# Another order for the last expert selection of an attention-then-MoE kernel, with one row group scaled by ScalarE

## The chip, the cores and the metric

The kernel runs on one core of a Trainium2 chip. The metric is the device time of one execution in microseconds (us); the time before is the median of three runs, 466.85 us (466.36 to 467.3). TensorE, VectorE, ScalarE and GpSimd compute; SyncE issues most DMAs, GpSimd the indirect ones (gathers and scatters by token number). In the profile they are PE (PEld for its weight loads), DVE, ACT, POOL and SP.

## What is computed

Causal attention over 8 batches, 12 heads, 448 tokens and head width 64, whose result (3584 tokens of 768 numbers) goes into a mixture of 8 experts. Each token picks one expert by the largest logit; an expert keeps the 80 tokens with the largest gate weight (its capacity) and drops the rest; a kept token gives its row times two matrices with a ReLU between, times its gate weight. All other output rows are zero.

```python
scores = scale * np.matmul(q, k.transpose(0, 1, 3, 2))      # then the causal mask
attn = np.exp(scores - max) / sum
x = (attn @ v), heads side by side                          # (3584, 768)
logits = x @ w_gate                                         # (3584, 8)
expert_idx = np.argmax(logits, axis=1)
gate_w = softmax(logits)[arange, expert_idx]
for e in range(8):
    tok_idx = the tokens with expert_idx == e, at most the 80 of the largest gate_w
    h = np.maximum(x[tok_idx] @ w1[e], 0.0)
    out[tok_idx] = gate_w[tok_idx, None] * (h @ w2[e])
```

## The kernel before

The work has three stages. The attention stage goes through 48 head pairs (8 batches of 6) in a software pipeline of 8 slots a pair; while one batch's heads are computed, the selection of the batch before it is spread over the slots. The expert stage takes the 8 experts one after the other: it gathers an expert's 80 rows from `xs` (the attention result in HBM), transposes them on TensorE, splits weights and rows into a high and a low half of 16 bits, and multiplies. A few chunks of the weights are not split but multiplied in 32 bits ("whole"); for expert 0 these are chunks 3 to 5 of the first matrix, and they come first.

Between the two lies the **tail**: the last batch has no attention left beside it, so its selection runs alone. Its order is written out by hand in the string `TAIL` (line 43): the names are taken from left to right, each calls one step, and each engine executes what the steps put into its queue in that order. The names that matter here:

- `r0w` to `r7w`: three TensorE transposes that turn a row group (128 or 64 tokens x 384 columns) of the last batch into rows (`row_group`, line 592). `r0e` to `r7e`: take them out of the accumulator banks. `r0m` to `r7m`: the scaling by the softmax's reciprocal sums, where another engine does it. One letter each in `ROW_ENGINES` (line 49) says who scales: `v` VectorE in one instruction (line 611), `a` ScalarE in six, one for each head (line 605), `p` a ScalarE copy (line 607) and then GpSimd (line 619). Scaled rows are written to `xs` by a DMA from SyncE's queue (line 615). Groups 3 and 7 are the ones of 64 tokens.
- `lg`, `logit`, `shifted`, `chosen`, `sums`, `one_hot`, `wsum`, `one_zero`, `wmore`, `weight`, `weighted`: logits, their maximum, the exponentials (`gex`, line 646, in the step `chosen`, on ScalarE), the one-hot of the expert and the gate weight, else on VectorE. `rest`: the left-over steps of the batch before, among them `tab` and `row` (lines 873 and 881, small ScalarE copies).
- `r0t`, `r0c`, `r1t`, `r1c`: one-hots and weights are transposed on TensorE (`selt`, line 731) and copied to `ex` by ScalarE (line 734).
- `rl`, `lt`, `cp`, `ro`: compare the 80 weights kept so far for each expert with those of the batch (lines 761, 767), count (line 774, "the counts' product") and make ranks (line 779).
- `c3w` to `c0w`: products that spread the batch's weights over 512, 384, 256 and 128 columns (`rn`, line 745); `c3l` to `c0l`: the comparisons on VectorE (`less`, line 748); `gt3` to `gt0`: counts of them (line 813).
- `places`, `places_more`, `earlier`, `own`, `rank`, `rr`, `tn`, `tab`: the one-hots of the places (`rm`, line 794), the tokens' ranks (`rank`, `rr`, lines 820 to 849), and the products `tn` (lines 859, 862) that sort token numbers and weights into the table. Out of it come `idx` (line 923), the token numbers for the gathers, and `gws`, the weights.
- `*n`: n matrix products without use (`wp`, line 1108) that keep TensorE busy.

Behind the tail ScalarE has eight weight splits in its queue (`wh`, line 1180), then `xw` and `xh` (lines 1220 and 1222), the gathered rows of expert 0 taken from the transposes `xtp` (line 1215). The first expert product (`hp`, line 1237) reads `xw`. The first gather (line 1197) waits for `idx` and for all writes to `xs`.

Of the kernel before, what the change touches and what calls it, by code (L numbers as in the profile page):

```python
# [41 lines left out]

TAIL = """
u ta ya tb yb v0 td yd tc yc v1 vy guard invert last_rows w gp0 wy close piece gp1 gs
r0w r0e r1w lp r1e r1m rest rest r2w r2e r3w r3e lg logit shifted chosen rest rest r4w r4e r5w *2
sums one_hot wsum one_zero wmore columns r0t r0c *3 weight weighted parts hold rl r1t r1c *1 lt r3m r4m r5e r5m cp ro r6w r6e r6m
c3w c3l c2w r7w r7e r7m c2l c1w gt3 *2 c0w c1l gt2 *1 c0l *1 gt1 places *1 earlier gt0 places_more own *5 rank rr tn tab *20
"""
ROW_ENGINES = "vpappppp"


@with_exitstack
def attention_then_moe(
# [928 lines left out]
    with tc.manual_schedule():  # L982
# [121 lines left out]
        def keep_warm(times):  # L1104

            wp = ps_v.tile([P, S], F32, name="wp", tag="xp")
            for _ in range(times):
                nc.tensor.matmul(wp, identb, before[:, 0:S], start=True, stop=True)
        for i, x in enumerate(ROW_ENGINES):
            g, t = divmod(i, NT)  # L1110
# [331 lines left out]
```

## Time and profile before

| | |
|---|---|
| median of three runs | 466.85 us (466.36 to 467.3) |
| the profiled execution | 466.07 us, span 464.2 us |
| TensorE busy, in the span | 441.8 us (95%) |
| VectorE, ScalarE, GpSimd busy | 413.1, 392.4, 310.3 us |
| DMA | 120.84 MB, mean 260 GB/s |
| TensorE from 340 to 350 us of the span | 9.55 us busy, clock 1.00, DMA share 0.27 |
| TensorE from 360 to 370 us | 10.00 us busy, clock 1.00, DMA share 1.01 |
| tail: last row transposes of the attention stage to the first expert product | 328.89 to 350.84 us |

Times inside the span count from its first instruction. In a timeline row stand start, length, engine, line, operation, names (out<-in), shapes and how many; in brackets follows how long the engine stood idle before it and who released it. Lengths of neighbours overlap by a little, so the distance of two starts is what an instruction costs in a queue; the length says when its result is there.

### The profile page before, as it was taken

The page shows a single profiled execution, that of the slowest core. Times are in us where ns is not written, and L with a number is a line of the kernel's source. Part 1 is how long each engine was busy: PE and PEld are TensorE (multiplying, and loading weights), DVE is VectorE, ACT ScalarE, POOL GpSimd, SP SyncE. Part 2 cuts the span into 40 slices and gives each one's busy share as a digit, 9 for nine tenths or more (in the row PEclk, how much of TensorE's full clock was granted, in tenths as well). Part 3 has the DMA queues.
Part 4 walks back from the last instruction along what each step waited for, and adds up shares of the span by engine and source line. Part 5 has one row for each costly group of instructions (what it writes and reads, how often), then busy time and mean ns, then how long its engine had stood idle before and what let it go on. Part 6 is the DMA issues. An engine that isn't in the chain of part 4 may idle for free.

```text
span 464.2 us, 14187 instructions
## 1 busy us (share of the span) xinstructions
PE 441.8 (95%) x4981; PEld 346.8 (75%) x4981; DVE 413.1 (89%) x1285; ACT 392.4 (85%) x1077; POOL 310.3 (67%) x382
## 2 busy tenths in 40 slices
PE   4899999999999999999999999999989999999994
PEld 2566667866777786677777767777648999999994
DVE  6888899988998999899899989989579999999892
ACT  6898989878988997898889789888586989988792
POOL 7999999988987987898798789860145133410011
PEclk9999999999999999999999999999999999999999
DMA  7758899989769578966957997539937999999941
GB/s 221 185 153 238 249 262 299 280 248 306 202 207 305 161 232 259 265 182 213 297 165 225 264 260 200 178 129 373 413 130 254 399 390 395 394 422 423 424 163 44
DMA packets 42998, 120.84 MB, mean 260 GB/s; under 512 B 6146, under 2 KB 23810, under 8 KB 39472
## 3 DMA queue, kind: packets, MB, share of 16 engines
q1 hardware_dynamic: 41712, 116.21, 76.9%
q0 software_dynamic: 1056, 3.51, 2.4%
q8 instruction: 39, 0.64, 0.6%
q14 instruction: 31, 0.25, 0.2%
q10 hardware_dynamic: 160, 0.23, 0.2%
HBM read 96.36 MB, written 23.99 MB: 259 GB/s over the span
## 4 chain that ended last, share of the span: by engine, by line
PE 83%; DVE 6%; DMA 3%; ACT 3%; issue 2%; SPq 1%; POOLq 0%; DVEq 0%
PE xp L495 16%; PE tp L465 15%; PE sp L423 6%; PE sp L424 5%; PE rt L592 4%; PE op L1245 4%; PE op L1237 4%; PE hp L1237 3%; PE gp L545 3%; PE hp L1252 3%; PE hp L1251 3%; PE hp L1249 3%; PE sp L433 3%; DMA qk<-k_t 3%; DVE ns L445 2%
## 5 line engine op out<-in xcount | busy, mean ns | idle before, releaser
L448 ACT ACTIVATE prob<-ns,nb 128x128 f32<-128x128 f32 (+3 forms) x336 | 177.0, 529 | 22.6 <-DVE nb L445 20.1
L445 DVE CUSTOM_DVE_ANT_0 ns<-sp,mask 128x384 f32<-128x384 f32 (+2 forms) x288 | 116.0, 413 | 18.7 <-PE sp L424 14.7
L465 PE MATMUL tp<-ident,prob 128*128 128x128 f32 x768 | 118.1, 276 | 0.9 <-ACT prob L448 0.9
L477 ACT COPY PT<-tp 128x512 f32<-128x512 f32 x182 | 104.0, 572 | 17.5 <-PE sp L423 8.4
L395 POOL TENSOR_TENSOR qk<-qk,qk 128x448 f16<-128x448 f32 x92 | 97.3, 1080 | 13.1 <-DVE qk L387 7.4
L465 PEld LDWEIGHTS tp<-ident,prob 128*128 128x128 f32 x768 | 89.6, 142 | 11.4 <-ACT prob L448 1.9
L1165 DVE SCALAR_TENSOR_TENSOR wl<-wraw,wh 128x768 f16<-128x768 f32 (+1 forms) x91 | 92.0, 1067 | 2.5 <-ACT wh L1180 2.3
L495 PE MATMUL xp<-PT,vt 128*64 128x448 f32 (+3 forms) x768 | 91.2, 380 | 0.0
L495 PEld LDWEIGHTS xp<-PT,vt 128*64 128x64 f32 x768 | 53.8, 137 | 42.7 <-issue 22.6
L423 PE MATMUL sp<-qk 128*128 128x384 f16 (+2 forms) x288 | 75.8, 279 | 8.0 <-DVE qk L349 5.1
L1180 ACT ACTIVATE wh<-wraw 128x768 f16<-128x768 f32 (+1 forms) x91 | 78.9, 931 | 4.2 <-PE hp L1252 1.8
L424 PE MATMUL sp<-qk 128*128 128x384 f16 (+2 forms) x288 | 78.1, 277 | 1.6 <-DVE qk L349 0.8
L448 ACT ACTIVATION_READ_ACCUMULATOR prob<-ns,nb 128x1 f32 x336 | 63.9, 190 | 0.0
L1338 POOL DMA_INDIRECT out<-yo,idx x8 | 14.6, 1828 | 69.0 <-ACT yo L1335 65.1
L390 POOL TENSOR_TENSOR qk<-qk,qk 64x448 f16<-64x448 f32 x46 | 54.2, 1179 | 3.4
L391 POOL TENSOR_TENSOR qk<-qk,qk 64x448 f16<-64x448 f32 x46 | 51.0, 1108 | 3.2
L387 DVE CAST qk<-qk 128x896 f16<-128x896 f32 x46 | 41.2, 897 | 1.1 <-DMA qk<-k_t 1.1
L423 PEld LDWEIGHTS <-qk 128*128 128x128 f16 x288 | 28.5, 99 | 17.1 <-issue 8.6
L384 POOL CAST qk<-qk 64x896 f16<-64x896 f32 x40 | 37.4, 936 | 4.3 <-PE sp L436 3.1
L1249 PEld LDWEIGHTS <-wh 128*128 128x128 f16 x362 | 36.5, 101 | 0.0
L1251 PEld LDWEIGHTS <-wh 128*128 128x128 f16 x362 | 36.2, 100 | 0.0
L1252 PEld LDWEIGHTS <-wl 128*128 128x128 f16 x362 | 36.2, 100 | 0.0
(192 smaller groups left out, 926.8 us busy)
## 6 DMA issues: line engine op xcount, KB each, us to landing
wraw<-w SPq DMA_DIRECT2D x27, 1536.0 KB, 20.4
qk<-k_t SPq DMA_DIRECT2D x92, 224.0 KB, 5.9
out<-mask_l SPq DMA_DIRECT2D x56, 192.0 KB, 4.4
qk<-q_t SPq DMA_DIRECT2D x23, 448.0 KB, 4.4
vt<-v_t SPq DMA_DIRECT2D x24, 384.0 KB, 5.9
xs<-xr SPq DMA_DIRECT2D x42, 192.0 KB, 3.9
wraw<-w SPq DMA_DIRECT2D x24, 256.0 KB, 6.1
vt<-v_t SPq DMA_DIRECT2D x24, 64.0 KB, 5.5
```

Of the source, the lines that this page charges most:

```text
L390: nc.gpsimd.tensor_tensor(out=qa[hi, i], in0=qf[lo, i], in1=qa[lo, i], op=ALU.subtract)
L391: nc.gpsimd.tensor_tensor(out=qb[lo, i], in0=qf[hi, i], in1=qb[hi, i], op=ALU.subtract)
L395: nc.gpsimd.tensor_tensor(out=k_lo[j][:, i], in0=kf[j][:, i], in1=k_hi[j][:, i], op=ALU.subtract)
L423: nc.tensor.matmul(sp[:, 0:w], qx[:, p, t * P:w], kx[:, p, 0:w], start=True, stop=False)
L424: nc.tensor.matmul(sp[:, 0:w], qx[:, p, t * P:w], lx[:, p, 0:w], start=False, stop=True)
L445: pr.masked = nc.vector.tensor_tensor_reduce(out=ns[:, 0:w], in0=sp[:, 0:w], in1=m, scale=-1.0 / 8.0, scalar=HUGE, op0=ALU.add, op1=ALU.mi ...
L448: nc.scalar.activation(pr.P[:, off:off + w], ns[:, 0:w], AF.Exp, bias=nb, scale=-1.0, accum_out=total)
L465: nc.tensor.transpose(pr.tp[:, i], pr.P[:, off:off + P], ident)
L477: copy(dst, src)
L495: state["pe"] = nc.tensor.matmul(xp[rows, 0:w], st["vt"][:, c, p * P + j * DH:p * P + (j + 1) * DH], pr.PT[:, j, n0:n0 + w], start=(c == 0 ...
L1165: return nc.vector.scalar_tensor_tensor(out=l, in0=src, scalar=SW, in1=h, op0=ALU.mult, op1=ALU.subtract)
L1180: nc.scalar.activation(h, src, AF.Copy, scale=SW)
```

## The change

Three things change in the hand-written order and one letter in `ROW_ENGINES`. The steps up to `chosen` come before the copies of row groups 2 and 3. The 512 columns' product and comparison come before the counts, and row groups 4 and 5 before both. The last row group, of 64 tokens, is scaled by ScalarE, in six instructions, instead of copied by ScalarE and scaled by GpSimd. Beside these the row groups 2, 3, 6 and 7 stand elsewhere, the comparison of 384 columns follows `ro`, the second `rm` and the first stand together behind `earlier`, and there are 40 products without use where there were 36. The core of the diff (its other lines are further names of the order):

```diff
-c3w c3l c2w r7w r7e r7m c2l c1w gt3 *2 c0w c1l gt2 *1 c0l *1 gt1 places *1 earlier gt0 places_more own *5 rank rr tn tab *20
+ro r6w r6e r6m c1w r7w r7e c2l *1 gt3 c0w c1l *1 gt2 *1 c0l gt1 earlier places gt0 places_more own *7 rank rr tn tab *20
...
-ROW_ENGINES = "vpappppp"
+ROW_ENGINES = "vpappppa"
```

On ScalarE, in the tail, from the small copy of the left-over step `tab` to the weight splits (`xrl` are the rows, `gex` the exponentials, `ex` the turned one-hots and weights, `wh` the splits), before:

```order
L873 CAST tab_0_678<-tn 80x40
L605 ACTIVATE xrl<-rt,sums 128x64 x6
L607 COPY xrl<-rt 64x384
L646 ACTIVATE gex<-gsh 128x32
L881 COPY row_0_682<-rp_6296 24x80
L607 COPY xrl<-rt 128x384
L734 COPY ex<-selt 24x512 x2
L607 COPY xrl<-rt 128x384 x2
L607 COPY xrl<-rt 64x384
L1180 ACTIVATE wh<-wraw 128x1024 x8
```

The same stretch of ScalarE's queue now:

```order
L873 CAST tab_0_678<-tn 80x40
L646 ACTIVATE gex<-gsh 128x32
L881 COPY row_0_682<-rp_6282 24x80
L605 ACTIVATE xrl<-rt,sums 128x64 x6
L734 COPY ex<-selt 24x512
L607 COPY xrl<-rt 64x384
L734 COPY ex<-selt 24x512
L607 COPY xrl<-rt 128x384 x3
L605 ACTIVATE xrl<-rt,rql 64x64 x6
L1180 ACTIVATE wh<-wraw 128x1024 x8
```

The exponentials stand ahead of the six scalings of group 2 and the copy of group 3; this copy stands between the two `ex` copies, the copies of groups 4, 5 and 6 behind the second; and where the copy of group 7 stood last, six scalings of 64x64 stand.

On TensorE, from the second `selt` to the counts (`rt` are row transposes, `rn` the columns' products, `cp` the counts, `wp` the products without use), the difference:

```order
 L731 MATMUL selt<-identb,mv 128x128
+L592 MATMUL rt<-ident,xu 128x128 x6
 L1108 LDWEIGHTS identb
 L1108 MATMUL wp<-before,identb 128x448
+L745 LDWEIGHTS ex
+L745 MATMUL rn<-ex 128x512
 L774 LDWEIGHTS lt
 L774 MATMUL cp<-oh_674,lt 80x8
```

And directly behind the last of the four `cp`:

```order
 L774 MATMUL cp<-oh_674,lt 80x8
-L592 MATMUL rt<-ident,xu 128x128 x3
-L745 LDWEIGHTS ex
-L745 MATMUL rn<-ex 128x512
 L745 LDWEIGHTS ex
 L745 MATMUL rn<-ex 128x384
```

The 512-column product moved from behind the four counts, and behind a row group, to ahead of them; row groups 4 and 5 moved ahead of it. Row group 6 now follows the 384-column product and row group 7 the 256-column one. On VectorE the 512-column comparison stands ahead of `ro`, and both `rm` behind the sum of `earlier`. SyncE's queue is the same, and GpSimd's lacks its fifth scaling.

More of the change, by code (lines that the diff above doesn't have):

```diff
@@ L44 @@
 u ta ya tb yb v0 td yd tc yc v1 vy guard invert last_rows w gp0 wy close piece gp1 gs
-r0w r0e r1w lp r1e r1m rest rest r2w r2e r3w r3e lg logit shifted chosen rest rest r4w r4e r5w *2
-sums one_hot wsum one_zero wmore columns r0t r0c *3 weight weighted parts hold rl r1t r1c *1 lt r3m r4m r5e r5m cp ro r6w r6e r6m
-c3w c3l c2w r7w r7e r7m c2l c1w gt3 *2 c0w c1l gt2 *1 c0l *1 gt1 places *1 earlier gt0 places_more own *5 rank rr tn tab *20
+r0w r0e r1w lp r1e r1m rest rest r2w lg logit shifted chosen rest rest r2e *3
+sums one_hot wsum one_zero wmore columns *3 r0t r0c r3w r3e *3 weight weighted parts hold rl r1t r1c r4w r5w *1 lt c3w r3m r4e r4m r5e r5m c3l cp c2w
+ro r6w r6e r6m c1w r7w r7e c2l *1 gt3 c0w c1l *1 gt2 *1 c0l gt1 earlier places gt0 places_more own *7 rank rr tn tab *20
 """
-ROW_ENGINES = "vpappppp"
+ROW_ENGINES = "vpappppa"
 @with_exitstack
```

## The prediction

> **What bounds the kernel now.** I read the page first, then the chain of waits from 322 us on, then who waited for whom in the expert stage, and last the engines' timelines between 333 and 352 us, where every edit lies.
>
> ```profile
> span 464.2 us, 14187 instructions
> ```
>
> The profiled execution took 466.07 us: this span and 1.87 us around it. It lies 0.78 us under the median of the runs shown (466.85). The sum below is a difference, so I add it to either.
>
> The chain of waits at the hand-over from the last selection to the experts (start, length, what):
>
> ```profile
> 346.51 0.16 DVE idx L923
> ...
> 346.96 3.17 DMA xg<-xs,idx
> ...
> 350.26 0.60 PE xtp L1215 x6
> 350.86 5.57 PE hp L1237 x48
> ```
>
> The list of token numbers (idx) releases the first gather, the gather releases the transposes of its rows, and these release the first expert product. From 350 us to the end TensorE waits for almost nothing; these are the only rows of its matmuls in the list of waits of that stretch (total, times, longest):
>
> ```profile
> PE xtp L1215 <- DMA xg<-xs,idx: 0.2, 1, 0.2
> ...
> PE ytp L1331 <- DVE yt L1311: 0.2, 1, 0.2
> ```
>
> So the expert stage is bound by TensorE, and what moves the first product, now at 350.86, moves the end by as much. The question is only what releases it. In the chain it is idx and the gather. But the product also needs xw, which ScalarE makes from the transposes, and ScalarE's queue reads (start, length, line, names, shapes, idle time before and its releaser):
>
> ```profile
> 336.01 1.34 ACT L605 ACTIVATE xrl<-rt,sums 128x64 f32<-128x64 f32 x6 [0.18 <-PE rt L592]
> 337.21 0.48 ACT L607 COPY xrl<-rt 64x384 f32<-64x384 f32 x1
> 337.57 0.25 ACT L646 ACTIVATE gex<-gsh 128x32 f32<-128x32 f32 x1
> 337.70 0.20 ACT L881 COPY row<-rp 24x80 bf16<-24x80 bf16 x1
> ...
> 340.21 0.57 ACT L734 COPY ex<-selt 24x512 bf16<-24x512 bf16 x1 [0.68 <-PE selt L731]
> 340.70 0.46 ACT L607 COPY xrl<-rt 128x384 f32<-128x384 f32 x1
> ...
> 342.30 0.47 ACT L607 COPY xrl<-rt 64x384 f32<-64x384 f32 x1 [0.22 <-PE rt L592]
> 342.67 7.68 ACT L1180 ACTIVATE wh<-wraw 128x1024 f16<-128x1024 f32 x8
> 350.55 0.44 ACT L1220 ACTIVATE xw<-xtp 128x80 f32<-128x80 f32 x2 [0.20 <-PE xtp L1215]
> ```
>
> Two things are to be seen. The exponential (L646) stands behind seven row operations. And between the last row copy and xw stand eight weight splits without a gap, after which ScalarE idles 0.20 us. That is all its slack: a second path, almost as late as the gather.
>
> **The exponential ahead of the rows.** VectorE's rows around it and on to the ranks:
>
> ```profile
> 336.65 0.19 DVE L641 TENSOR_TENSOR gsh<-logit,gmx 128x32 f32<-128x32 f32 x1
> ...
> 337.32 0.19 DVE L659 TENSOR_TENSOR goh<-goh,gfm 128x32 f32<-128x32 f32 x1
> 337.85 0.18 DVE L665 TENSOR_REDUCE ggw<-gex 128x4 f32<-128x32 f32 x1 [0.34 <-ACT gex L646]
> ...
> 339.46 0.19 DVE L716 TENSOR_TENSOR mv<-grest,mv 128x32 bf16<-128x32 f32 x1
> ...
> 341.21 0.22 DVE L779 TENSOR_SCALAR ro<-cp,pnum 80x8 f16<-80x8 f32 x1 [0.29 <-PE cp L774]
> 341.81 0.75 DVE L748 SCALAR_TENSOR_TENSOR less<-rn,ggw,before 128x512 bf16<-128x512 f32 x1 [0.38 <-PE rn L745]
> ...
> 343.43 0.34 DVE L748 SCALAR_TENSOR_TENSOR less<-rn,ggw,before 128x128 bf16<-128x128 f32 x1
> 343.70 0.08 DVE L748 DVE_READ_ACCUMULATOR less<-rn,ggw,before 128x1 f32 x1
> 343.70 0.48 DVE L794 TENSOR_TENSOR rm<-ro,slots_e 80x320 bf16<-80x320 f16 x1
> ...
> 345.40 0.49 DVE L849 TENSOR_TENSOR rr<-rank,slots_t 128x320 bf16<-128x320 f16 x1
> ```
>
> gsh ends at 336.84; the exponential can begin some 0.04 later and end by 337.13, before VectorE is through with L659 at 337.51. The 0.34 us wait goes; the one-hots and all that follow come 0.34 earlier, L716 (what the second selt reads) ending at 339.31. What is late next is TensorE, by its own queue:
>
> ```profile
> 338.53 0.40 PE L731 MATMUL selt<-identb,oh 128*128 128x128 bf16 x4 [1.13 <-DVE oh L702]
> 338.76 0.73 PE L1108 MATMUL wp<-before,identb 128*128 128x448 bf16 x3
> 339.59 0.32 PE L761 MATMUL rl<-row,ex 128*128 128x80 bf16 x4
> 339.79 0.38 PE L731 MATMUL selt<-identb,mv 128*128 128x128 bf16 x4
> 340.01 0.35 PE L1108 MATMUL wp<-before,identb 128*128 128x448 bf16 x1
> 340.31 0.86 PE L774 MATMUL cp<-oh,lt 128*80 128x8 bf16 x4
> 341.03 0.53 PE L592 MATMUL rt<-ident,xu 128*128 128x128 f32 x3
> 341.39 0.54 PE L745 MATMUL rn<-ex 128*128 128x512 bf16 x2
> 341.77 0.49 PE L592 MATMUL rt<-ident,xu 128*128 128x128 f32 x3
> ```
>
> Pitches, from one start to the next: 0.23 for four selt, 0.36 for three row transposes, 0.20 for four rl; three wp end 0.73 after their start against 0.35 for one, so 0.19 each. The first selt starts at 338.53 - 0.34 = 338.19. Three row transposes are now put behind it, so rl follows at 338.19 + 0.23 + 0.36 + 3 x 0.19 = 339.35 (before 339.59): 0.24 is left of the 0.34. The six scalings of the third row group now stand between exponential and first ex copy: 336.88 + 0.23 for the two small operations, then 1.20 (336.01 to 337.21), free at 338.31; selt is there at 338.59. They are hidden by 0.3 us; without that cover they would cost what exceeds it.
>
> **The 512 columns ahead of the counts.** The second selt runs at 339.55 and its ex copy ends at 339.55 + 0.38 + 0.04 + 0.57 = 340.54 (the copy of a row group between the two ex copies ends by 339.6). TensorE meanwhile does two row groups and one wp, 339.55 + 0.22 + 2 x 0.36 + 0.19 = 340.68, and takes the 512-column product then, not at 341.39: 0.71 earlier. The first comparison moves from 341.81 to 341.10. Two things are given back. The ranks ro (0.22 long) now lie behind it: 0.10, taken midway between nothing (wholly overlapped) and its length. And the sum after the last comparison has no rm to cover its accumulator read any more (rm started at 343.70, the read ended at 343.78): 0.12 with the hand-over. So rr starts at 345.40 - 0.71 + 0.10 + 0.12 = 344.91 and the gather 0.49 earlier. The wp in front of tn, seven where there were five, begin when the last comparison is done, about 343.2, and are through by 344.7, before rr ends. The gather's transposes would start at 349.77 and, were they the last thing, the product at 350.37.
>
> **The last row group on ScalarE.** Where its transposes stand on TensorE: the 512- and the 384-column product took 0.38 together (341.39 to 341.77), the counts take some 0.22 when VectorE no longer paces them (estimate from the four rl), three transposes 0.36, the 256-column product some 0.11 by its share of the 0.38: 340.68 + 0.38 + 0.22 + 0.36 + 0.11 = 341.75, against 341.77 now. So ScalarE gets the last row group when it did, at 342.28. Then, in place of one copy after which the next instruction started 0.37 later (342.30 to 342.67), come six scalings. The trace has none of 64x64; the nearest row is the 128x64 one, 1.20 for six. Half the partitions do not help: 64x384 and 128x384 copies take 0.48 and 0.46. Bounds are six times 0.32 without any overlap, 1.9, and half the row's price, 0.6. I take 1.20: the weight splits begin at 343.48, 0.81 later, and xw, the ninth in that queue, is reached 0.81 later too. Of this the 0.20 idle time and some 0.10 of overlap between neighbours (the copy ended at 342.77, the split began at 342.67) are covered: xw starts at 351.06 where it was 350.55, and the first product about 351.37. **The path has changed hands: the gather comes 0.49 earlier, the product 0.51 later.** The two price bounds make it -0.1 and +1.2.
>
> The Trainium skill, page "ScalarE: Activation LUTs", section "What ACT_TABLE_LOAD costs", gives an ACTIVATE with one pointer operand 280 ns + 0.833 ns per column, neighbours overlapping by 93 ns; an estimate from it is 0.24 a piece, 1.44 for six, and the sum would be 0.75 where the rows give 0.51. Its "Rules for kernel authors" sends multiplications to VectorE and not to ScalarE, which speaks against this edit; the trace's 0.20 is a little cheaper than the page's figure.
>
> **GpSimd and the row writes.** GpSimd loses its fifth scaling:
>
> ```profile
> 340.44 2.54 POOL L619 TENSOR_TENSOR xrl<-xrl,sums 128x384 f32<-128x384 f32 x3
> 342.94 0.82 POOL L619 TENSOR_TENSOR xrl<-xrl,rql 64x384 f32<-64x384 f32 x1
> 346.96 1.08 POOL L1197 DMA_INDIRECT xg<-xs,idx  x1 [3.19 <-DVE gws L930]
> ...
> DMA to landing us min/median/max: 1.8/1.9/1.9
> ...
> xs<-xr SPq DMA_DIRECT2D x42, 192.0 KB, 3.9
> ```
>
> These are two stretches of its timeline and the gather, the landing times of the eight row writes of this stage, and the page's row for the earlier row writes. Now its chain of three ends at 342.98 and the write of the last row group follows 343.76. Afterwards the three start when their first copy is done, about 340.95, and end at 343.5; the last scaling ends at 342.28 + 1.34 = 343.62. The two last writes go out of SyncE's queue at 343.5 and about 343.85: the last as now. At the 1.9 us that these eight writes took, it lands at 345.75, and the gather, which waits for it, needs it at 346.18. Hidden, by 0.4 us where it was 0.9.
>
> **Rivals.** *The gather's path still decides.* If ScalarE reached xw by 350.06, the product would follow the transposes: -0.49, 466.36 us. The six scalings would have to cost no more than the copy did, and the eight splits to run 0.5 shorter, as they could if part of their 7.68 is waiting that the trace does not tell from work; with the first alone it is about -0.3. For it: the chain of now runs through idx. Against: the 1.20 in the row and splits that follow each other every 0.96. 0.10. *The row writes decide.* If the last write takes the 3.9 us of the earlier row writes (last row above) instead of 1.9, it lands at 347.75 and the gather starts 0.3 later, 348.05, against 346.96: +1.1, 467.95 us, slower. It decides from a landing of 2.3 us on. For it: the write is the last of eight and its slack is halved. Against: all eight took 1.8 to 1.9. 0.08. *The gain and the delay are lost in the expert stage,* its queue of splits absorbing the shift, so that 466.85 stays: 0.10; against it, TensorE has no gap there that could take it up.
>
> **The numbers.** The forecast, xw held up by ScalarE's queue, has 0.72: +0.5, that is 466.57 against the profiled 466.07, and 467.35 against the median 466.85, or +0.11%. A measurement of this kernel can tell about 0.2% (0.93 us) from no change. The forecast (to about +0.8 with a late last transpose), the first and the third rival lie mostly within it. Slower takes the second rival and the tail of the forecast, 0.13; faster only what a lucky set of runs would add to the first rival, 0.04; same 0.83. The range takes in the first rival with half the spread of the runs below it, and the second above: 466.1 to 468.0.
>
> **What would show it.** Right: the exponential right behind gsh and no wait at L665; the 512-column comparison near 341.1; idx about 0.5 earlier; six L605 of 64x64 before the splits; xw released not by the transposes but by the splits, with TensorE idle about 1 us between the gather's transposes and the first product. Wrong: a first product before 350.86, or a gather that waits for the row writes.

## The result, and the profile after

The changed kernel takes 471.78 us (median of 6 runs, 470.41 to 472.54), the kernel before 467.08 us beside it (6 runs, 466.01 to 468.74): a ratio of 1.0095, 95% interval 1.007 to 1.012. It is slower by some 4.4 us, where 467.35 was forecast, at most 468.0. The profiled execution took 470.71 us; the page:

```profile
span 468.9 us, 14200 instructions
```

**Where the time went.** First the table of stretches, TensorE's busy time in three of them (stretch, length, then busy time and count of PE, PEld, DVE, ACT and POOL, the clock, the DMA share and GB/s). Before:

```profile
350.00:356.00 6.00, 5.81 (x53) 5.63 (x53) 5.36 (x6) 4.00 (x8) 3.44 (x2) 1.00 0.85 296
356.00:362.00 6.00, 6.00 (x159) 6.00 (x159) 5.84 (x9) 4.13 (x8) 1.17 (x1) 1.00 1.01 343
362.00:372.00 10.00, 10.00 (x165) 10.00 (x161) 10.00 (x14) 9.86 (x17) 1.74 (x1) 1.00 1.01 397
```

After:

```profile
350.00:356.00 6.00, 4.48 (x41) 4.34 (x41) 3.97 (x5) 5.09 (x9) 4.43 (x3) 1.00 0.77 264
356.00:362.00 6.00, 3.83 (x69) 3.71 (x69) 3.49 (x5) 1.26 (x3) 0.96 (x1) 1.00 0.99 285
362.00:372.00 10.00, 9.23 (x205) 9.08 (x202) 10.00 (x12) 9.08 (x15) 0.00 (x0) 1.00 1.02 388
```

TensorE idles 1.52 + 2.17 + 0.77 = 4.46 us in these 22 us, where it idled 0.19. The loss is three gaps behind the selection, at the clock of before; nothing in the selection itself has become longer. TensorE's rows at these places and the last entries of the list of waits:

```profile
351.56 0.61 PE L1215 MATMUL xtp<-ident,xg 80*128 80x80 f32 x6 [1.52 <-ACT wh L1180]
352.14 5.59 PE L1237 MATMUL hp<-xw,wraw 128*128 128x80 f32 x48
359.90 0.61 PE L1215 MATMUL xtp<-ident,xg 80*128 80x80 f32 x6 [2.17 <-DMA xg<-xs,idx]
```

```profile
PE xtp L1215 <- DMA xg<-xs,idx: 2.2, 1, 2.2
...
PE hp L1237 <- issue: 0.8, 1, 0.8
```

The first gap, ahead of the first expert's transposes, is put down to a weight split of ScalarE, the eighth, which ends at 351.45. But in the kernel before the transposes started at 350.26, while the eighth split still ran (342.67 + 7.68 = 350.35), so they don't need it. What they wait for is the landing of the first gather's rows, 0.14 us ahead of them in both kernels (350.12 and 351.42). The second gap is the second expert's gather; the third stands in the second expert's products and waits for nothing that the profile shows.

**The selection did what was forecast.** VectorE's rows after (start, length, line, names, shapes, idle before):

```profile
338.00 0.18 DVE L665 TENSOR_REDUCE ggw<-gex 128x4 f32<-128x32 f32 x1
...
341.44 0.75 DVE L748 SCALAR_TENSOR_TENSOR less<-rn,ggw,before 128x512 bf16<-128x512 f32 x1 [0.32 <-PE rn L745]
...
346.48 0.16 DVE L923 TENSOR_TENSOR idx<-xf,tn 80x8 int32<-80x8 f32 x1
...
346.96 0.16 DVE L931 TENSOR_TENSOR gws<-gws,sv 80x8 f32<-80x8 f32 x1
347.15 3.50 DVE L1165 SCALAR_TENSOR_TENSOR wl<-wraw,wh 128x1024 f16<-128x1024 f32 x3
```

The two executions differ by 0.58 us ahead of the first changed name of the order, which no changed code explains. The start of the gate product shows it, first before, then after:

```profile
332.23 1.74 PE L545 MATMUL gp<-xu,wgd 128*32 128x448 f32 x12
```

```profile
332.81 1.70 PE L545 MATMUL gp<-xu,wgd 128*32 128x448 f32 x11
```

So in what follows "from the gate product" is the start minus 332.23 before, and minus 332.81 after; the experiments use each run's own start. L665 no longer waits. The 512-column comparison starts at 8.63 (before 9.58), idx at 13.67 (before 14.28): 0.61 earlier, where 0.49 was forecast. VectorE's first weight split (`wl`, L1165) follows this list at 14.34, also 0.61 earlier (before 347.18, 14.95).

**The gather did not come earlier by as much.** GpSimd after, and beside it the second gather of before (its first stands in the prediction):

```profile
347.29 2.03 POOL L1197 DMA_INDIRECT xg<-xs,idx  x1 [3.49 <-DVE gws L931]
349.63 1.84 POOL L1197 DMA_INDIRECT xg<-xs,idx  x1 [0.31 <-issue]
```

```profile
348.34 0.96 POOL L1197 DMA_INDIRECT xg<-xs,idx  x1 [0.31 <-issue]
```

The first gather starts at 14.48 from the gate product, where it was 14.73: 0.25 earlier, not 0.61. It takes 2.03 us, not 1.08, and the second starts 0.71 us later from the gate product (16.82, before 16.11; 1.29 later in the span). The row names `gws` as the releaser, which had ended before; where several are waited for, the records tell them apart. The records of GpSimd's sequencer, finer than the views, show when its wait for the last row write ends. Before, that is at 345.89, idx is done at 346.67, and the gather starts 0.29 behind idx. After, the row write's wait ends at 346.33, idx is done at 346.64, and the gather starts 0.96 behind the row write. The same 0.96 stands in other runs, such as the one with the unscaled rows below (346.11 to 347.07). So before, the row write was hidden by 0.11 us only (345.89 + 0.96 = 346.85, against 346.96). The row write is the 96 KB one in the DMA view of the changed kernel (342 to 348 us; issues, KB each, us to landing):

```profile
xs<-xrl SPq DMA_DIRECT2D x3, 192.0 KB, 1.8
xs<-xrl SPq DMA_DIRECT2D x1, 96.0 KB, 2.1
```

**What the order did.** The gather is now 0.14 us behind VectorE's first split (347.29 and 347.15); before it was 0.22 ahead (346.96 and 347.18). What followed is in the chain of waits after:

```profile
349.63 10.14 DMA xg<-xs,idx
359.76 0.14 issue
359.90 0.61 PE xtp L1215 x6
```

The second gather takes 10.14 us to land. The DMA view of the two stretches 348 to 351.6 and 351.6 to 354.9 us says why. Queue q0 carries the gathers (64 packets each), q1 the weights. Before, one row of each stretch:

```profile
q0 software_dynamic: 128, 0.28, 27.2%
...
q1 hardware_dynamic: 90, 1.11, 97.7%
```

After:

```profile
q0 software_dynamic: 64, 0.03, 3.7%
...
q1 hardware_dynamic: 88, 1.08, 98.9%
```

Before, both gathers' packets had moved when a 1.5 MB weight load began (its first packet at 351.73 in the trace's DMA records). After, the weight load began at 351.63, when only the first gather's had; the second gather's moved from 355.0 on, in among the load, and had landed by 359.77.

From the gate product the load, too, has moved: 18.82, where it was 19.50. SyncE issues it when VectorE's third split is done, at 350.73 before and 350.65 after; its rows, first before, then after:

```profile
350.76 0.34 SPq L202 DMA_DIRECT2D wraw<-w  x1
```

```profile
350.67 0.34 SPq L202 DMA_DIRECT2D wraw<-w  x1
```

So the earlier splits brought the load 0.68 forward while the second gather fell 0.71 back. The second gather is held as the first was: it starts at 349.63, 0.20 behind the third split, and its issue ends at 351.47, 0.83 behind this split's end and 0.16 ahead of the load's first packet. Before, its issue had ended at 349.30, 2.43 ahead of the load.

**The ledger**, first product and later marks, after minus before: ahead of the change 0.58; first transposes +0.72 (350.26 to 351.56, 1.30 with these 0.58); second transposes +2.33 (356.27 to 359.90, 3.63 in all); the gap in the second expert's products +1.02 (4.65 at the third transposes, and constant from there on). 0.58 + 0.72 + 2.33 + 1.02 = 4.65, the spans' 4.7.

### The profile page after: what moved, and what is told of

The parts are those of the page before. It is cut to its first block, busy times and chain, and to the rows that moved or that the text cites. A ratio compares the mean times of both kernels' runs of the same rounds, so it can differ in the third digit from the quotient of the medians.

```text
span 468.9 us, 14200 instructions
## 1 busy us (share of the span) xinstructions
PE 442.4 (94%) x4985; PEld 347.1 (74%) x4985; DVE 413.6 (88%) x1285; ACT 393.6 (84%) x1082; POOL 301.4 (64%) x381
## 4 chain that ended last, share of the span: by engine, by line
PE 81%; DVE 6%; DMA 6%; issue 2%; ACT 2%; SPq 0%; POOLq 0%; ACTq 0%; POOL 0%; DVEq 0%
PE xp L495 17%; PE tp L465 15%; PE sp L423 6%; PE sp L424 5%; PE rt L592 4%; PE op L1245 4%; DMA qk<-k_t 4%; PE op L1237 3%; PE gp L545 3%; PE sp L433 3%; PE hp L1251 3%; PE hp L1249 3%; PE hp L1252 3%; PE hp L1237 2%; DMA xg<-xs,idx 2%
## 5 line engine op out<-in xcount | busy, mean ns | idle before, releaser
L1165 DVE SCALAR_TENSOR_TENSOR wl<-wraw,wh 128x768 f16<-128x768 f32 (+1 forms) x91 | 92.0, 1066 | 2.6 <-ACT wh L1180 2.5
L1338 POOL DMA_INDIRECT out<-yo,idx x8 | 9.4, 1174 | 74.2 <-ACT yo L1335 70.3
```

The source lines that it names most:

```text
L1165: return nc.vector.scalar_tensor_tensor(out=l, in0=src, scalar=SW, in1=h, op0=ALU.mult, op1=ALU.subtract)
```

## The theories

A is the forecast's: ScalarE's six scalings delay xw. R: the row write's landing delays the gather, and the loss is that delay. C: the *order of two starts*. A gather that starts while a VectorE split runs doesn't advance until this split ends; so the first gather's start behind the split costs some 0.95 us, the second gather is 0.7 later, and the weight load's packets then go ahead of the second gather's.

The Trainium skill, page "GPSIMD Engine Reference", section "1. Specifications", says that GpSimd's SBUF interfaces are shared with VectorE, with contention for VectorE's instructions that have two SBUF inputs. The split reads two (`wraw` and `wh`), and the trace agrees that the gather is held, 2.03 us against 1.08. In four runs a gather started inside L1223, a VectorE instruction that reads `xtp` from the accumulator banks and so has one SBUF input; it took 0.95 to 0.96 us, as one that meets nothing. That it is the shared port that holds the gather, no run here shows.

## The experiments

Twelve kernels, each timed beside the kernel before. "Changed +" starts from the changed kernel, "before +" from the one before.

**Changed + VectorE's splits later.** Three small additions, each dependent on the one before, ahead of the first split; nothing else is touched.

```diff
 nc.vector.tensor_tensor(out=g[0:sn], in0=g[0:sn], in1=sv[0:sn, 2], op=ALU.add)
+for _ in range(3):
+    last_of.append(nc.vector.tensor_tensor(out=sv[0:sn, 1], in0=sv[0:sn, 1], in1=sv[0:sn, 2], op=ALU.add))
```

> The changed kernel with three tiny dependent additions (80x8, about 0.2 us each) on VectorE behind the gate weights, so that its first weight split starts some 0.6 us later, at about 347.75 instead of 347.15 of the span. Theory C (the order of two starts): the loss comes from the first gather starting behind VectorE's first split, which stretches GpSimd's work on the gather from 1.08 to 2.03 us and pushes the second gather behind a weight load. Then the first gather takes 1.0 to 1.2 us again, the second starts about 1 us earlier and lands ahead of the weight load, TensorE's waits of 2.2 and about 0.8 us in the first two experts go, and the time falls by 2.5 to 4 us, to 468 to 469.3. Theory R (the row writes alone are late and all else follows one to one): no gain, 471.8 to 472.4. Theory A (ScalarE's queue holds xw, as forecast): no gain, 471.8.

467.41 us (466.38 to 468.7, 10 runs), ratio 1.0004 (0.9989 to 1.0019). Its GpSimd and VectorE rows:

```profile
348.20 1.08 POOL L1197 DMA_INDIRECT xg<-xs,idx  x1 [3.48 <-DVE sv L931]
349.58 1.09 POOL L1197 DMA_INDIRECT xg<-xs,idx  x1 [0.31 <-issue]
```

```profile
347.97 0.62 DVE L931 TENSOR_TENSOR sv<-sv 80x8 f32<-80x8 f32 x3
348.61 3.50 DVE L1165 SCALAR_TENSOR_TENSOR wl<-wraw,wh 128x1024 f16<-128x1024 f32 x3
```

The gather, at the same place from the gate product (14.47), is ahead of the split and takes 1.08; the second gather's packets (351.39 to 352.72) are ahead of the first weight packet (353.11); no gap at the second transposes. *More* work for VectorE takes the whole loss away, more than the 2.5 to 4 us that were expected. This is C; A and R would have kept it. The additions hold the weight load too (19.38 from the gate product, not 18.82), so this run alone doesn't separate the two steps of C.

**Before + the gather later.** The converse: a small GpSimd copy ahead of the first gather.

```diff
 ii = keep.tile([SL, E], I32, name=f"idx{s}")
+nc.gpsimd.tensor_copy(keep.tile([SL, 1], F32, name="late"), xf[0:SL, 0:1])
```

> The kernel before with one tiny copy on GpSimd (80x1, reads the tile from which the token numbers are made) ahead of the first gather, so that this gather starts 0.3 to 0.6 us later, behind VectorE's first weight split instead of 0.22 us ahead of it. Nothing else is changed. Theory C: the first gather takes about 2 us instead of 1.08, the second starts over 1 us later and misses the gap ahead of the weight load; 3 to 4.5 us slower, 470 to 471.6. Theories R and A: the delay is handed on one to one, 0.3 to 0.6 us, 467.4 to 467.7.

473.7 us (473.29 to 474.5, 4 runs), ratio 1.0141 (1.0124 to 1.0158). GpSimd, and the table of stretches:

```profile
348.21 1.67 POOL L1197 DMA_INDIRECT xg<-xs,idx  x1 [0.96 <-DVE gws L931]
350.19 1.85 POOL L1197 DMA_INDIRECT xg<-xs,idx  x1 [0.31 <-issue]
```

```profile
360.00:367.00 7.00, 6.48 (x97) 6.51 (x98) 4.06 (x6) 3.43 (x6) 0.96 (x1) 0.53 0.98 377
```

The split starts at 347.71, the gather 0.50 behind it; it takes 1.67 and again ends some 0.94 us after the split (347.71 + 1.23 = 348.94, 349.88). The loss is there without a line of the change, and larger than the change's: from 359.73, inside the gap ahead of the second transposes, the granted clock is at a half for 6.8 us. That was not foreseen.

**Before + ScalarE scales the last rows.** The letter alone, and with it the name `r7m`, GpSimd's step, which falls away.

```diff
-c3w c3l c2w r7w r7e r7m c2l
+c3w c3l c2w r7w r7e c2l
-ROW_ENGINES = "vpappppp"
+ROW_ENGINES = "vpappppa"
```

> The kernel before with the last row group scaled by ScalarE in six instructions, and nothing else of the change. Theory A: the weight splits begin about 0.8 us later and the first product 0.5 us later: 467.6. Theory C: the last row write lands within 0.2 us of where it did and the first gather still starts ahead of the first split, so that the gathers keep their lengths and only the 0.5 us of theory A is left. If the six scalings alone made the loss: 470 to 472.

467.75 us (466.43 to 468.92, 10 runs), ratio 1.001 (0.9996 to 1.0023). TensorE:

```profile
350.87 0.61 PE L1215 MATMUL xtp<-ident,xg 80*128 80x80 f32 x6
352.28 5.58 PE L1237 MATMUL hp<-xw,wraw 128*128 128x80 f32 x48 [0.80 <-ACT xw L1220]
```

Here A's mechanism is seen by itself: transposes on time, product held by xw, 19.18 from the gate product where it was 18.61, so +0.57. It is real in the trace, and an eighth of the loss; the total times do not resolve it.

**Changed + GpSimd scales the last rows again.** The order of the change, without the letter.

```diff
-ROW_ENGINES = "vpappppa"
+ROW_ENGINES = "vpappppp"
-r7w r7e c2l
+r7w r7e r7m c2l
```

> The changed kernel with the last row group copied by ScalarE and scaled by GpSimd as before, all else as changed. Theory A: the weight splits on ScalarE begin 0.8 us earlier than in the changed kernel; where its queue was the cause most of the loss goes. Theory C: the last row write lands later still by 0.4 to 0.7 us (GpSimd's scalings end at about 344.6), the first gather starts behind the first split again, and the loss stays: 471 to 473.

467.44 us (466.52 to 468.23, 10 runs), ratio 1.0002 (0.9991 to 1.0012): C's expectation missed. Its VectorE and GpSimd rows:

```profile
344.05 0.75 DVE L821 TENSOR_TENSOR rank<-number_after,parts 128x4 f16<-128x4 f32 x1
...
347.93 3.50 DVE L1165 SCALAR_TENSOR_TENSOR wl<-wraw,wh 128x1024 f16<-128x1024 f32 x3
```

```profile
343.96 0.82 POOL L619 TENSOR_TENSOR xrl<-xrl,rql 64x384 f32<-64x384 f32 x1
...
347.85 1.08 POOL L1197 DMA_INDIRECT xg<-xs,idx  x1 [3.07 <-DVE gws L930]
```

What was missed is that GpSimd can hold VectorE as well. L821 (two SBUF inputs) started 0.09 us behind GpSimd's scaling, took 0.75 us where it takes 0.16, and ended with it (344.80 and 344.78). All of VectorE's work behind it came 0.6 later, the split too; the gather was 0.08 ahead of it again and took 1.08. The expectation was wrong in where the split would fall, and the rule of the order held.

**Changed + one addition.** As the first, with one addition in place of three.

> The changed kernel with one tiny dependent addition (80x8, about 0.2 us) on VectorE ahead of its first weight split, where the earlier run had three. The split then starts some 0.05 us behind the start of the first gather instead of 0.14 us ahead of it. Theory C (only the order of the two starts counts): 0.2 us of added work bring back most of the 4.4 us, 467 to 468.5, with a first gather of about 1.1 us. If the gain of three additions came from room between the two and not from their order: about a third of it, 470 to 471. Theory R: no gain.

471.0 us (469.41 to 472.07, 4 runs), ratio 1.0096 (1.007 to 1.0122). The split stayed at 14.34 from the gate product: the one addition went into a pause that was there already. So it tells nothing of the theories and is a repeat of the changed kernel, at the same loss.

**Changed + the last two row groups unscaled.** Groups 6 and 7 are copied and written; *their scaling is left out*.

```diff
-ROW_ENGINES = "vpappppa"
+ROW_ENGINES = "vpappp--"
```

> The changed kernel, but the last two row groups are written as ScalarE copies them (their scaling by the softmax sums is left out), so that their writes no longer wait for GpSimd's fourth scaling or ScalarE's six. The last write then goes out about 0.8 us earlier; VectorE's queue is untouched. Theory C with the row writes as the cause of the late start: the first gather is released by the token numbers again, starts 0.29 us behind them and so about 0.2 us ahead of the first split, takes 1.1 us, and TensorE's waits in the first experts go: 466.5 to 467.8. If the late start has another cause than the landing of the writes (the token numbers, GpSimd's own sequencer): the gather still starts behind the split, 471 to 472.5.

466.15 us (465.95 to 467.41, 10 runs), ratio 0.9991 (0.998 to 1.0003).

```profile
347.07 1.08 POOL L1197 DMA_INDIRECT xg<-xs,idx  x1 [3.97 <-DVE gws L930]
```

The split is at 347.16. The last row write landed at 346.11 in the sequencer's records, the gather started 0.96 later, 0.09 ahead of the split, and took 1.08. The write was 0.3 earlier from the gate product and not 0.8, so it still set the gather's start, which was expected of idx. The first product comes at 17.98 from the gate product, 0.63 earlier than before: this is the selection's gain, seen whole. So the landing of the row write is what put the gather behind the split, R's part of C.

**Changed + the last rows on VectorE.** An attempt at a version better than both: the last row group scaled by VectorE behind its last comparison.

```diff
-ROW_ENGINES = "vpappppa"
+ROW_ENGINES = "vpappppv"
-r7w r7e c2l *1 gt3 c0w c1l *1 gt2 *1 c0l gt1 earlier
+r7w c2l *1 gt3 c0w c1l *1 gt2 *1 c0l r7e gt1 earlier
```

> The changed kernel with the last row group scaled by VectorE in one instruction behind the last comparison, where VectorE waits 0.1 us anyway. ScalarE's queue gets shorter by 0.8 to 1.2 us, GpSimd's stays short, and the token numbers and the first split both come about 0.45 us later. Theory C: the first gather, at the token numbers plus 0.29 us, starts about 0.2 us ahead of the first split, and the loss goes; the first product stands some 0.2 us earlier from the start of the tail than in the kernel before: 466.3 to 467.3, which is no difference that can be measured from the kernel before. Theory A: only ScalarE's part of the delay goes: 471 to 471.5.

467.13 us (466.09 to 467.7, 12 runs), ratio 1.0004 (0.9993 to 1.0015). The gather is 0.11 ahead of the split (347.23 and 347.34), and the first product 0.24 earlier than before, from the gate product; it makes no difference that can be measured. No version here beat the kernel before.

**Changed + the first weight load later.** For C's second step: the weight load that gets in front of the second gather is held until the gathers are issued.

```diff
+behind = hold[0] if len(wload) == WBUF + WMORE and hold else behind
 t, src = piece()
...
-gather(nx)
+load_piece.__defaults__[1].append(gather(nx))
```

> The changed kernel, with the first weight load of the expert stage held until GpSimd has issued its first four gathers (about 4 us later); first gather and first split are as in the changed kernel. If the second gather lands late because this load of 1.5 MB is ahead of its packets: the first gather stays at about 2 us, the second lands by about 353 us and not at 360, TensorE's wait of 2.2 us for it goes, and the time falls by 2 to 3.4 us, to 468.4 to 469.8. If the stretched work on GpSimd alone makes it late: no change, 471 to 472.5. If the held load is missed later on: slower.

473.59 us (468.57 to 474.33, 4 runs), ratio 1.0111 (1.007 to 1.0153). The wait at the second transposes was gone, but TensorE ran at half its clock, as the table of stretches shows:

```profile
354.00:360.00 6.00, 6.00 (x30) 6.00 (x30) 5.15 (x5) 1.86 (x3) 0.42 (x2) 0.50 0.91 298
```

TensorE was idle from 350.35 to 351.92, ahead of the first transposes, and the granted clock was at a half for 13.65 us from 352.99. Three runs had a mean clock of 0.978 to 0.982 and took 473.35 to 474.33 us; the one at 0.998 took 468.57. The median cannot decide on the second step, so the last two runs kept TensorE busy.

**Changed + more products without use.** 28 in place of 20 in the last filling, which reach to the gather's landing.

```diff
-own *7 rank rr tn tab *20
+own *7 rank rr tn tab *28
```

> The changed kernel with more products without use (28 in place of 20 a step) in the last filling of TensorE's wait for the gather, which reach to about the gather's landing. If idle TensorE ahead of the first expert lets the granted clock fall in some runs of the changed kernel, and this adds to its loss: the granted clock is 0.994 or more in each run, and 469.8 to 471 us. The rest of the loss, 3 to 4 us, stays by theory C, since the gather still starts behind the split and takes 2.03. If the clock has no part: 471.8.

470.24 us (469.15 to 472.9, 5 runs), ratio 1.0086 (1.0051 to 1.0121), mean clocks 0.991 to 0.997. Against the 0.994 that was expected of all runs this is a half miss: the gap ahead of the first transposes is filled, the one ahead of the second (1.33 us in the list of waits) is not. The loss stays, 3 to 4 us (the medians differ by 3.3, the ratio gives 4.0), and the gather still takes 2.04.

**Both: more products and the weight load later.**

> The row with the first weight load held behind the gathers, with 28 products without use in place of 20 in the last filling. The first weight load then doesn't stand ahead of the second gather's packets, and the clock should not fall. Theory C's second step (the second gather is late because the weight load's packets went ahead of its own, 2.3 us at the second transpose): 468 to 469.5 us at a granted clock of 0.994 or more, 2 to 3 below the changed kernel. If the weight load ahead of the second gather has no part in the loss: 471 or more.

468.23 us (467.23 to 471.67, 10 runs), ratio 1.0032 (1.0012 to 1.0051); nine of the ten runs have clocks of 0.995 or more.

```profile
347.18 2.01 POOL L1197 DMA_INDIRECT xg<-xs,idx  x1 [3.51 <-DVE gws L931]
349.50 1.84 POOL L1197 DMA_INDIRECT xg<-xs,idx  x1 [0.31 <-issue]
```

```profile
351.39 0.61 PE L1215 MATMUL xtp<-ident,xg 80*128 80x80 f32 x6
...
357.40 0.58 PE L1215 MATMUL xtp<-ident,xg 80*128 80x80 f32 x6
```

The gathers are as late and as long as in the changed kernel. But the second gather's packets move from 352.04 on, ahead of the first weight packet at 356.45, and the second transposes wait for nothing. It takes 2.0 us less than the run above, from which it differs in the held load alone: C's second step, by itself. The whole gain against the changed kernel is some 3 us (the ratios differ by 0.0063), while the first gather's collision remains.

**Changed + two additions.** Between the one, which moved nothing, and the three.

> The changed kernel with two small dependent additions of VectorE ahead of its first weight split (the row with three moved the split by enough, the one with one addition did not move it). Theory C (the order of two starts: a gather that starts behind a VectorE split waits for that split's end): the split starts some 0.2 to 0.3 later, the first gather 0.05 to 0.15 ahead of it, the gather then takes 1.08 and not 2.03, the second gather's packets move ahead of the first weight packet, 467 to 468 us. If what counts is the distance between the two and not their order: the gather is shortened in part only, some 469 to 470. If the loss were ScalarE's (theory A) or the row writes' alone (theory R): 471 to 472, since neither is touched.

467.71 us in the median of 10, ratio 1.0044 (1.001 to 1.0077). The profiled run:

```profile
347.55 1.08 POOL L1197 DMA_INDIRECT xg<-xs,idx  x1 [3.51 <-DVE sv L931]
```

Its split is at 347.66, 0.11 behind the gather. The ten times tell more than their median: seven lie from 466.84 to 467.81, three from 470.83 to 473.33, none between. With the two starts 0.1 apart one or the other comes first, and the price is paid whole or not at all. An effect of the distance would have given times between. The three were not profiled, so that the order was turned in them is argued, not shown. Against it stands that three other kernels have the two starts as near in their profiled runs (0.08 to 0.11) and none of their 32 times lies above 468.3.

**Before + the three additions.** A control.

> A control: the kernel before with the three small additions ahead of its first weight split. Theory C: the gather is ahead of the split in the kernel before already, so its length stays at 1.08 and the second gather's packets stay ahead of the first weight packet; the split's own delay is hidden or costs up to 0.4: 467.0 to 467.6 us. If a pause of VectorE were a gain by itself: some 4 us below the kernel before, 463.

467.78 us (466.65 to 468.63, 10 runs), ratio 1.001 (0.9995 to 1.0024). The pause is no gain by itself; it helps only where it turns the order.

**The order in all fourteen kernels.** Start of the first gather minus start of the first split, and the gather's length (us), from the rows of each:

```
changed + 28, load later +0.16 2.01    before + scalar rows   -0.22 1.08
changed + load later     +0.16 2.02    before                 -0.22 1.08
changed                  +0.14 2.03    changed + vector rows  -0.11 1.08
changed + one addition   +0.14 2.03    changed + two add.     -0.11 1.08
changed + 28             +0.14 2.04    changed + unscaled     -0.09 1.08
before + gather later    +0.50 1.67    changed + GpSimd rows  -0.08 1.08
                                       changed + three add.   -0.41 1.08
                                       before + three add.    -0.69 1.08
```

Without an exception: ahead of the split, 1.08; behind it, the rest of the split and 0.94 more. The step lies between -0.08 and +0.14. Later gathers of the same traces narrow it: one that started 0.02 behind a split (the second before, and with the scalar rows) was not held, one that started 0.04 behind (the fourth after) was.

This order is not the loss itself. In four kernels without a loss the second gather is held as well, by the second split, and takes 1.9 us ("changed +" GpSimd rows, unscaled, vector rows and two additions). What tells all the kernels apart is where the second gather's issue ends: 0.16 to 0.18 us ahead of the weight load's first packet in the four that lose and have the load in its place, 1.49 us or more ahead in the eight that don't. A first gather behind the first split puts the second behind the third split, whose end also releases the load.

## Why the prediction was wrong

*The exponential, the 512 columns:* right. The wait at L665 is gone, idx is 0.61 earlier where 0.49 was forecast.

*The last row group on ScalarE:* right in size. The six of 64x64 take 1.19 us to the first split, and 1.20 was taken:

```profile
342.57 1.31 ACT L605 ACTIVATE xrl<-rt,rql 64x64 f32<-64x64 f32 x6
343.76 7.69 ACT L1180 ACTIVATE wh<-wraw 128x1024 f16<-128x1024 f32 x8
351.85 0.44 ACT L1220 ACTIVATE xw<-xtp 128x80 f32<-128x80 f32 x2 [0.40 <-PE xtp L1215]
```

The row decides here against the estimate of 1.44 that the prediction drew from the Trainium skill, page "ScalarE: Activation LUTs", section "What ACT_TABLE_LOAD costs". The group's transposes came 0.29 earlier than forecast, so the splits are 0.51 later from the gate product, not 0.81. And the last row shows that xw waited for the transposes, with ScalarE idle for 0.40: not ScalarE but the gather set the first product. So "the path has changed hands" failed; that the product came 0.72 later, near the 0.51 of the forecast, is chance.

*The row writes, the step that failed:* "the gather, which waits for it, needs it at 346.18. Hidden, by 0.4 us". The landing itself was forecast to 0.01 us (345.75 - 332.23 = 13.52 from the gate product, measured 346.33 - 332.81 = 13.52). But the gather starts 0.96 us after a landing, and 0.29 only after idx. The prediction took the 0.3 for both. That the landing came out so well is luck: the write was issued 0.19 earlier than forecast and took 0.2 longer. The 1.9 us were never this write's: the landing times in the prediction leave it out, and before it took 2.1 as well (issued at 343.79, its wait over at 345.89). So the rival "decides from a landing of 2.3 us on" should have read: idx ends at 13.83 and would let the gather start at 14.12, 0.96 before that is 13.16, and the write was issued at 11.4; from 1.8 us on. The write took 2.1. For the 0.96 the profile had the sign, the wait of GpSimd's sequencer, but in the changed kernel only; before, idx came last and hid it.

*"The gather comes 0.49 earlier" was not worth 0.49.* The second error is larger. Each path was followed by itself, the selection's gain going to all that waits for it alike. It did not: the split took all of its 0.61, the weight load behind it 0.68, the gather 0.25, and gather and split changed places. No sentence of the prediction looks at what VectorE runs when the gather starts, nor at which DMA stands in front of the second gather, and with them the loss has no place in the sum. The rival that it names for a slower kernel has the right place, the row write, but prices only the delay itself, +1.1 at the most; in the runs without the collision (unscaled rows, vector rows) tenths there are worth tenths.

*The range:* of the 4.4 us, 0.72 is the collision's delay of the first product, 2.33 the second gather behind the weight load, 1.02 the gap in the second expert's products, together 4.07; the clock in some runs fits the rest. The third gap stays open. It is also in runs that lose nothing (0.8 us of "issue" with the GpSimd rows, 0.9 with the vector rows), so the order does not make it; before has none. In several runs it stands at the same count of TensorE's weight loads from the start of the program, and 16 KB of instructions are fetched shortly before, which would fit a late fetch; no run tested that.

## What to carry to other kernels

When a step becomes faster, list everything that is released by it, and compare the new starts of neighbours on different engines: a gain of 0.6 us handed on unevenly can turn the order of two starts, and the order may be worth more than the gain. For each wait that a cover hides, look for the price behind that kind of event: here 0.96 us after a DMA's landing and 0.29 after another engine's instruction, and only the one that comes last is to be seen. Where a small DMA is needed soon, ask which large load will stand in front of it if it comes a microsecond late.

## What the runs showed of the hardware

- A VectorE split with two SBUF inputs holds a gather's issue on GpSimd: the first gather took 1.08 us when it started ahead of a 1.23 us split, and 1.67 to 2.04 when it started behind, in all fourteen kernels. The reverse was not seen: a split that started 0.08 us or more behind a gather took its usual 1.22 to 1.23. GpSimd's own scaling, though, held a VectorE instruction of 0.16 us for 0.75.
- The second gather, of 64 packets, landed in 9.4 to 10.2 us where its issue ended 0.2 us ahead of a 1.5 MB weight load's first packet, and in 3.5 to 5.9 where it was further ahead.
- The granted clock fell to a half for 13.65 us, 1.1 us behind an idle time of TensorE of 1.57, and for 6.8 us within one of 2.30. After a gap of 2.17, in the changed kernel's profiled run, it did not fall. The Trainium skill, page "TensorE: Matmul & The Clock Gate", section "Part 1: The HAM clock gate", puts an idle window of about 3.4 us ahead of the slow state; the gaps here were shorter, and by that row no clock would have been lost.
